# Moving and stationary tiles placed 192 bytes apart modulo 256 in an attention and two-layer expert kernel

## The chip, the cores and the metric

One NeuronCore of a Trainium2 chip runs the whole program. The metric is the device time of one execution in microseconds; the time before is 1484.91 us, the median of three runs (1484.45 to 1487.26).

## The reference

```python
# attention over keys and values averaged in groups of 8 (576 -> 72), for 8 batches and 8 heads of 64
scores = q @ mean8(k).T / 8;  attn = softmax(scores);  x = attn @ mean8(v)     # q, k, v: (8, 8, 576, 64)
x = x.transpose(0, 2, 1, 3).reshape(4608, 512)
# part one: three-way maximum, then a projection, d_ff = 768
h = maximum(maximum(x @ w1, x @ w2), x @ w3);  x = h @ w_out                    # 512 -> 768 -> 512
# part two: squared relu, d_ff = 2048
return ((relu(x @ w_in) ** 2) @ w_out)                                          # 512 -> 2048 -> 512
```

All inputs are float32; the weights arrive as 64-bit values that the kernel converts.

## The kernel before

Every large matrix product is made of three products of split values: an operand is cut into a high part (rounded to `float32r`) and the remainder, and high times high, high times low and low times high are summed in PSUM (`PARTS`). Each tile of activations or weights therefore has two halves, index 0 and 1. A matmul instruction names a stationary operand of 128 columns, which TensorE loads first (the profile's PEld rows), and a moving operand that is streamed past it (the PE rows). Every matmul has its own load.

Part one runs over 12 blocks of 384 tokens (`moe1`). A block does 18 products of 12 matmuls (L521: six chunks of the hidden layer times three weights; stationary `w1`, moving `x`, 384 columns) and 4 products of 18 matmuls (L540; stationary `wo1`, moving `h`). In a product the moving tile changes after every three matmuls. Attention for the next block (L361 to L421) and the preparation of part two's weights are woven between these steps by a table of due times.

Part two runs over 9 blocks of 512 tokens in a seven-product scheme on 2x2 blocks. `product` (L676) multiplies one of seven combinations of the activations, `y1` to `y7` (moving, 256 columns), with weights `wi2s` (stationary), 12 matmuls each. `moe2_out` (L806) has it the other way round: the split hidden values `g` are stationary and the output weights `wo2s`, fetched through a ring of five buffers, are the moving operand, 256 columns, again 12 matmuls with one `g` and one `wo2s`. Both lines have 3024 matmuls in all.

A scheduler sets the order of the instructions of every engine. Tiles are laid out by pools, one after the other along a partition of SBUF. What matters below is where a tile starts modulo 256 bytes; all slices of one tile that matmuls use start at the same place modulo 256, since the steps inside a tile are multiples of 512 bytes. Called *the difference* from here on: start of the moving operand minus start of the stationary operand, modulo 256. Before the change a helper, `shifted` (L90), allocates 16 floats more than a tile needs, so that neighbouring buffers of `x`, `h`, `y` and `wo2s` start 64 bytes apart modulo 256. Laid out by the pools, the starts modulo 256 are:

| operand | line | role | start before | difference before (matmuls) |
|---|---|---|---|---|
| `x` | L521 | moving | 160, 96, 32, 224 in turn | 0, 192, 128, 64 (648 each) |
| `w1`, `wo1` | L521, L540 | stationary | 160 | |
| `h` | L540 | moving | 160, 224, 96, 32 | 0 (300), 64 (276), 192 (156), 128 (132) |
| `y1` to `y7` | L676 | moving | 32, 32, 160, 96, 224, 96, 160 | 0 (864), 128 (864), 192 (810), 64 (486) |
| `wi2s` | L676 | stationary | 160, the first pair's half 32 | |
| `wo2s` | L806 | moving | 64, 64, 0, 192, 128 over the ring | 192 (1224), 0, 64, 128 (600 each) |
| `g` | L806 | stationary | 128 | |

So in L521 the difference changes after every three matmuls, and in part two it stays for stretches of 4 to 24 matmuls, since the scheduler weaves products in pieces of 4, 8 and 12.

Of the kernel before, what the change touches and what calls it, by code (L numbers as in the profile page):

```python
# [10 lines left out]
F32 = mybir.dt.float32  # L11
F32R = mybir.dt.float32r
# [8 lines left out]
P = 128  # L21
# [12 lines left out]
T1 = 384  # L34
# [29 lines left out]
AHEAD = 2  # L64
# [18 lines left out]
def as_f32(ap):  # L83
    return ap.bitcast(F32)


SHIFT = 16


def shifted(pool, shape, **names):  # L90

    n = 1
    for s in shape[1:]:
        n *= s
    t = pool.tile([P, n + SHIFT], F32R, **names)
    axes = " ".join(f"a{i}" for i in range(len(shape) - 1))
    return t[:, :n].rearrange(f"p ({axes}) -> p {axes}", **{f"a{i}": s for i, s in enumerate(shape[1:])})


@with_exitstack  # L100
def attention_moe_kernel(ctx: ExitStack, tc: tile.TileContext, q, k, v, vn, w1, w2, w3, wo1, wi2, wo2, out):
# [42 lines left out]
    def split(hl, src, engine=nc.vector):  # L144

        split_to(hl[:, 0], hl[:, 1], src, engine)
# [39 lines left out]

    w_p = s1.enter_context(tc.tile_pool(name="w_p", bufs=1))
    x_p = s1.enter_context(tc.tile_pool(name="x_p", bufs=2 * KD))
    h_p = s1.enter_context(tc.tile_pool(name="h_p", bufs=KF1))
    t_p = s1.enter_context(tc.tile_pool(name="t_p", bufs=2))  # L190

# [3 lines left out]
    sm_p = s_at.enter_context(tc.tile_pool(name="sm_p", bufs=4, side="right"))  # L195
    pt_p = s_at.enter_context(tc.tile_pool(name="pt_p", bufs=2, side="right"))
    xf_p = s_at.enter_context(tc.tile_pool(name="xf_p", bufs=1, side="right"))
    ah_p = s_at.enter_context(tc.tile_pool(name="ah_p", bufs=AHEAD, side="right"))
    sc_ps = s_at.enter_context(tc.tile_pool(name="sc_ps", bufs=2, space=PSUM))
    tr_ps = s_at.enter_context(tc.tile_pool(name="tr_ps", bufs=1, space=PSUM))  # L200
# [23 lines left out]
    unused = list(spare)  # L224
# [55 lines left out]
    x_t = {}  # L280
# [46 lines left out]
    def attend(j, b, s0, n, p, t):  # L327
# [23 lines left out]
        m = tiles[0][1]  # L351
# [46 lines left out]

        def values():
            if t == 0:  # L400
                x_t[j][p] = shifted(x_p, [P, 2, T1], tag="x", name="x")
            x = x_t[j][p][:, :, t : t + n]
            if whole:
                av = av_ps.tile([P, T1], F32, tag="av0", name="av0")[:, :n]
                for h in range(2):
                    nc.tensor.matmul(
                        av, lhsT=vst_f[p // 2][:, p % 2, h : h + 2].rearrange("p a d -> p (a d)"), rhs=pt[0][:, h, :n],
                        start=(h == 0), stop=(h == 1),
                    )
                split(x, av)  # L410
                return
            hi, lo = pt[0][:, 0, :, :n], pt[0][:, 1, :, :n]
            xf = xf_p.tile([P, T1], F32, tag="xf", name="xf")[:, :n]
            for h in range(2):
                av = av_ps.tile([P, T1], F32, tag=f"av{h}", name=f"av{h}")[:, :n]
                lhsT = vst[:, p, 2 * h : 2 * h + 2].rearrange("p a d -> p (a d)")
                nc.tensor.matmul(av, lhsT=lhsT, rhs=hi[:, h], start=True, stop=False)  # L417
                nc.tensor.matmul(av, lhsT=lhsT, rhs=lo[:, h], start=False, stop=True)  # L418
                r, o = slice(h * D, (h + 1) * D), slice((1 - h) * D, (2 - h) * D)
                nc.scalar.activation(xf[r], av[o], AF.Copy)  # L420
                nc.vector.tensor_tensor(out=xf[r], in0=av[r], in1=xf[r], op=ALU.add)  # L421
            split(x, xf)
# [86 lines left out]
    def moe1(j):  # L509

        x = x_t.pop(j)
        hs = []
        for f in range(KF1):
            hm = t_p.tile([P, T1], F32, tag="hm", name="hm")
            h = shifted(ah_p if j == 1 and f < AHEAD else h_p, [P, 2, T1], tag="h", name="h")
            for e in range(NE):
                ps = mm_ps.tile([P, T1], F32, tag="ps", name="ps")
                n = 0
                for kk in range(KD):
                    for a, c in PARTS:  # L520
                        nc.tensor.matmul(  # L521
                            ps, lhsT=w1_t[f, e][:, a, kk * P : (kk + 1) * P], rhs=x[kk][:, c],
                            start=(n == 0), stop=(n == 3 * KD - 1),
                        )
                        n += 1
                if e == 0:
                    nc.scalar.activation(hm, ps, AF.Copy)
                else:
                    nc.vector.tensor_tensor(out=hm, in0=ps, in1=hm, op=ALU.max)  # L529
                if e == NE - 1:  # L530
                    split(h, hm)
                yield
            hs.append(h)
            now[0] = hm
        for d in range(KD):
            ps = mm_ps.tile([P, T1], F32, tag="ps", name="ps")
            n = 0
            for kk in range(KF1):
                for a, c in PARTS:
                    nc.tensor.matmul(  # L540
                        ps, lhsT=wo1_t[kk][:, a, d * P : (d + 1) * P], rhs=hs[kk][:, c],
                        start=(n == 0), stop=(n == 3 * KF1 - 1),
                    )
                    n += 1
            ys = t_p.tile([P, T1], F32, tag="ys", name="ys")
            nc.scalar.activation(ys, ps, AF.Copy)
            nc.scalar.dma_start(out=y_dram[j][d], in_=ys)
            yield
# [6 lines left out]
    def add_moe1(j):  # L555
        steps = moe1(j)
        for i in range(STEPS):
            when = j * STEPS + i
            if j == 1 and i < NE * AHEAD:
                when = NE * KF1 + i * KD / (NE * AHEAD)  # L560
            todo.append((when, functools.partial(next, steps, None)))
# [31 lines left out]
    NG = NP2 // 2  # L593
    HT = T2 // 2
    y_p = ctx.enter_context(tc.tile_pool(name="y_p", bufs=1, side="right", reuse_waits="tile"))
    w2_p = ctx.enter_context(tc.tile_pool(name="w2_p", bufs=1, side="right", reuse_waits="tile"))
    wi2_t, wo2_t, yr_t, y_t = {}, {}, {}, {}

# [5 lines left out]
            wi2_t[p].append(w)  # L604

    def fetch_out(gr, m, h):
        w = shifted(wo_p, [P, 2, 2, 256], tag="wo2", name="wo2s")
        nc.sync.dma_start(out=as_f32(w), in_=wo2_dram[m, gr % 2, h])
        wo2_t.setdefault((gr, m, h), []).append(w)

# [30 lines left out]
    def split_y(j, m):  # L641
        src = y_t[j]
        if m == 4:
            src[4] = yr_t[j, 1, 0]
            nc.vector.tensor_tensor(out=src[4], in0=src[4], in1=as_f32(src["t6"]), op=ALU.subtract)
        if m == 6:
            src["t6"] = src[6]
        y = shifted(y_p, [P, 2, 2, HT], tag=f"y{m}", name=f"y{m}")
        split(y, src[m])
        src[m] = y  # L650

    ORDER = (1, 6, 7, 5, 2, 4, 3)
    early = [functools.partial(load_y, 0), functools.partial(mix_y, 0)]
    early.append(functools.partial(fetch_in, 0, w2_p))
    early += [functools.partial(split_y, 0, m) for m in ORDER]
    for i, f in enumerate(early):
        todo.append(((NB1 - 1) * STEPS + (i + 0.5) * (NE * KF1) / len(early), f))
# [4 lines left out]
    c_p = ctx.enter_context(tc.tile_pool(name="c_p", bufs=1, reuse_waits="tile"))  # L662
    w3_p = ctx.enter_context(tc.tile_pool(name="w3_p", bufs=1, reuse_waits="tile"))
    wo_p = ctx.enter_context(tc.tile_pool(name="wo_p", bufs=5, reuse_waits="tile"))
    for pool in (w3_p, wo_p):
        pool.tile([P, SHIFT // 2], F32, name="shift")
    acc_ps = ctx.enter_context(tc.tile_pool(name="acc_ps", bufs=1, space=PSUM, reuse_waits="tile"))

    def product(bank, j, gr, m, first=False):
# [145 lines left out]
    def fetch_group(gr):  # L815
        for m, h in OUT[gr >= NG // 2]:
            fetch_out(gr, m, h)
# [5 lines left out]
    for j in range(NB2):  # L823
        for gr in range(NG):
            more = j + 1 < NB2
            c = moe2_in(j, gr)

            ready = list(ORDER) if gr == NG - 1 and more else []
            for n, (m, h) in enumerate(OUT[gr >= NG // 2]):
                if n == 6 and ready:  # L830
                    mix_y(j + 1)
                if n >= 6:
                    for y in ready[2 * n - 12 : 2 * n - 10]:
                        split_y(j + 1, y)
                moe2_out(j, gr, m, h, c)
            if gr == NG - 2 and more:
                load_y(j + 1)
            nxt = j * NG + gr + 1
            if nxt < NB2 * NG:
                fetch_group(nxt % NG)  # L840
# [41 lines left out]
```

## Time and profile before

| | |
|---|---|
| median of three runs | 1484.91 us |
| the profiled execution | 1485.27 us |
| its span, first to last instruction | 1483.5 us |
| PE busy | 1452.1 us, 98% of the span |
| PEld, DVE, ACT, POOL busy | 96%, 66%, 52%, 12% |
| granted TensorE clock, mean over the span | 0.993 |
| part one, first matmul of L521 to last of L540 | 27.7 to 757.7 us |
| part two, L676 and L806 | 757.9 us to the end |

Matmuls overlap: the profile models the end of each, so a row's "mean ns of one" is longer than the step from one matmul's start to the next. The step is read from the timeline, as the distance of two rows' starts divided by the count.

### The profile page before, as it was taken

The page shows a single profiled execution, that of the slowest core. Times are in us where ns is not written, and L with a number is a line of the kernel's source. Part 1 is how long each engine was busy: PE and PEld are TensorE (multiplying, and loading weights), DVE is VectorE, ACT ScalarE, POOL GpSimd, SP SyncE. Part 2 cuts the span into 40 slices and gives each one's busy share as a digit, 9 for nine tenths or more (in the row PEclk, how much of TensorE's full clock was granted, in tenths as well). Part 3 has the DMA queues.
Part 4 walks back from the last instruction along what each step waited for, and adds up shares of the span by engine and source line. Part 5 has one row for each costly group of instructions (what it writes and reads, how often), then busy time and mean ns, then how long its engine had stood idle before and what let it go on. Part 6 is the DMA issues. An engine that isn't in the chain of part 4 may idle for free.

```text
span 1483.5 us, 27579 instructions
## 1 busy us (share of the span) xinstructions
PE 1452.1 (98%) x10410; PEld 1429.8 (96%) x10410; DVE 985.1 (66%) x1778; ACT 764.6 (52%) x1983; POOL 180.2 (12%) x228
## 2 busy tenths in 40 slices
PE   6889999999999999999999999999999999999998
PEld 4879999999999999999999999999999999999998
DVE  5896466675675756755426767676867767686765
ACT  7795365665666656654224544453635344454443
POOL 3441022312222212222000000000000000000000
PEclk9999999999999999999999999999999999999999
DMA  6643135533444433324369748475656666565746
GB/s 224 190 162 103 54 132 158 174 97 133 159 148 141 135 127 119 108 100 152 112 235 340 270 139 291 140 266 189 223 192 216 223 227 223 203 205 186 265 135 220
DMA packets 118307, 263.94 MB, mean 178 GB/s; under 512 B 12672, under 2 KB 62848, under 8 KB 118176
## 3 DMA queue, kind: packets, MB, share of 16 engines
q1 hardware_dynamic: 111264, 252.75, 50.4%
q10 hardware_dynamic: 6912, 9.44, 1.7%
q8 instruction: 82, 1.34, 0.4%
q14 instruction: 49, 0.40, 0.1%
HBM read 213.91 MB, written 48.23 MB: 177 GB/s over the span
## 4 chain that ended last, share of the span: by engine, by line
PE 90%; DMA 4%; ACT 3%; DVE 2%; issue 1%; POOL 0%; DVEq 0%; ACTq 0%; SPq 0%; POOLq 0%
PE ps L521 28%; PE ps L676 24%; PE ps L540 10%; PE accB L806 7%; PE accA L806 6%; PE accF L806 3%; PE accE L806 3%; PE accD L806 3%; PE sc L361 2%; DMA wo2s<-wo_dram 2%; PE tr L389 2%; ACT ss L366 1%; PE av L418 1%; DMA wraw<-in_w_dram 1%; PE av L417 1%
## 5 line engine op out<-in xcount | busy, mean ns | idle before, releaser
L521 PE MATMUL ps<-x,w 128*128 128x384 f32 x2592 | 496.1, 343 | 4.0 <-ACT w L141 1.3
L521 PEld LDWEIGHTS ps<-x,w 128*128 128x128 f32 x2592 | 451.9, 189 | 6.8 <-ACT w L141 3.0
L676 PE MATMUL ps<-y,wi2s 128*128 128x256 f32 x3024 | 378.8, 280 | 0.3
L676 PEld LDWEIGHTS ps<-y,wi2s 128*128 128x128 f32 x3024 | 365.6, 188 | 1.3 <-DVE a L686 0.6
L540 PE MATMUL ps<-h,wo 128*128 128x384 f32 x864 | 161.8, 339 | 0.2 <-ACT wo L141 0.2
L540 PEld LDWEIGHTS ps<-h,wo 128*128 128x128 f32 x864 | 149.6, 188 | 0.9 <-ACT wo L141 0.5
L686 DVE TENSOR_TENSOR c<-ps,c 128x512 f32<-128x512 f32 x144 | 98.4, 688 | 73.8 <-PE ps L676 72.5
L695 ACT ACTIVATE c<-c 128x512 f32<-128x512 f32 x90 | 55.7, 627 | 172.5 <-DVE c L686 170.3
L529 DVE TENSOR_TENSOR hm<-ps,hm 128x384 f32<-128x384 f32 x144 | 79.5, 552 | 69.4 <-PE ps L521 67.0
L141 ACT ACTIVATE g<-c 128x512 fp32r<-128x512 f32 x144 | 90.4, 627 | 59.2 <-DVE c L692 23.8
L806 PE MATMUL accB<-wo2s,g 128*128 128x256 f32 x864 | 115.5, 281 | 5.0 <-DMA wo2s<-wo_dram 3.5
L806 PE MATMUL accA<-wo2s,g 128*128 128x256 f32 x864 | 119.3, 280 | 0.0
L806 PEld LDWEIGHTS accB<-wo2s,g 128*128 128x128 f32 x864 | 107.3, 188 | 6.5 <-ACT g L141 3.2
L142 DVE TENSOR_TENSOR g<-c,g 128x512 fp32r<-128x512 f32 x144 | 98.6, 685 | 19.1 <-ACT g L141 19.1
L806 PEld LDWEIGHTS accA<-wo2s,g 128*128 128x128 f32 x864 | 109.6, 189 | 0.0
L366 ACT ACTIVATE ss<-sc,st 128x72 f32<-128x72 f32 (+1 forms) x320 | 97.9, 320 | 16.6 <-DVE st L363 14.1
L372 POOL TENSOR_TENSOR ss<-ss,st 128x432 f32<-128x432 f32 (+1 forms) x64 | 56.4, 881 | 261.7 <-DVE st L371 188.5
L421 DVE TENSOR_TENSOR xf<-av,xf 64x192 f32<-64x192 f32 (+1 forms) x112 | 50.7, 453 | 47.0 <-ACT xf L420 45.0
L393 DVE TENSOR_TENSOR pt<-tr,pt 72x192 fp32r<-72x192 f32 (+1 forms) x112 | 49.4, 450 | 41.2 <-ACT pt L392 39.4
L420 ACT ACTIVATE xf<-av 64x192 f32<-64x192 f32 (+1 forms) x112 | 45.4, 405 | 54.9 <-PE av L418 39.7
L141 ACT ACTIVATE h<-hm 128x384 fp32r<-128x384 f32 x72 | 37.6, 522 | 66.4 <-DVE hm L529 65.8
L141 ACT ACTIVATE g<-s 128x512 fp32r<-128x512 f32 x72 | 45.0, 630 | 45.4 <-DVE s L689 25.9
(105 smaller groups left out, 1980.8 us busy)
## 6 DMA issues: line engine op xcount, KB each, us to landing
wo2s<-wo_dram SPq DMA_DIRECT2D x252, 512.0 KB, 5.0
wi2s<-wi_dram SPq DMA_DIRECT2D x24, 512.0 KB, 9.0
wraw<-in_wo_dram SPq DMA_DIRECT2D x22, 512.0 KB, 4.3
wraw<-in_w_dram SPq DMA_DIRECT2D x18, 512.0 KB, 3.5
y_dram<-ys ACTq DMA_DIRECT2D x48, 192.0 KB, 2.0
wraw<-in_wi_dram SPq DMA_DIRECT2D x16, 512.0 KB, 3.8
wi_dram<-wraw SPq DMA_DIRECT2D x16, 512.0 KB, 3.6
wo_dram<-wraw SPq DMA_DIRECT2D x64, 128.0 KB, 2.0
```

The lines of the kernel that those rows point to most:

```text
L141: nc.scalar.activation(hi, src, AF.Copy)
L142: engine.tensor_tensor(out=lo, in0=src, in1=as_f32(hi), op=ALU.subtract)
L366: nc.scalar.activation(ss[:, i, h], src[:, i, h], AF.Exp, bias=st[:, 0, i, h : h + 1], accum_out=st[:, 1, i, h : h + 1],)
L372: nc.gpsimd.tensor_tensor(out=ss, in0=ss, in1=st[:, 2].rearrange("p g (h o) -> p g h o", o=1).to_broadcast([m, g, 2, SP]), op=ALU.mult,)
L421: nc.vector.tensor_tensor(out=xf[r], in0=av[r], in1=xf[r], op=ALU.add)
L521: nc.tensor.matmul(ps, lhsT=w1_t[f, e][:, a, kk * P : (kk + 1) * P], rhs=x[kk][:, c], start=(n == 0), stop=(n == 3 * KD - 1),)
L529: nc.vector.tensor_tensor(out=hm, in0=ps, in1=hm, op=ALU.max)
L540: nc.tensor.matmul(ps, lhsT=wo1_t[kk][:, a, d * P : (d + 1) * P], rhs=hs[kk][:, c], start=(n == 0), stop=(n == 3 * KF1 - 1),)
L676: nc.tensor.matmul(bank[:, u * HT : (u + 1) * HT], lhsT=wi2_t[2 * gr + u][i][:, a, o + kk * P : o + (kk + 1) * P], rhs=y_t[j][m][:, c, kk] ...
L686: nc.vector.tensor_tensor(out=out, in0=in0, in1=in1, op=ALU.add)
L695: nc.scalar.activation(c, c, AF.Relu)
L806: nc.tensor.matmul(bank[:, i * 256 : (i + 1) * 256], lhsT=g[:, a, u * HT + i * P : u * HT + (i + 1) * P], rhs=w[:, u, c], start=(n == 0 an ...
```

## The change

Instead of a longer tile, each pool gets one small tile that nothing uses (`leave`), which pushes what follows by 32 to 192 bytes. The tiles have their plain lengths again, all multiples of 512 bytes, so that all buffers of a pool start at the same place modulo 256. The starts become: `x` and `h` 96 against `w1` and `wo1` 160; `y1` to `y7` 224 against `wi2s` 32; `wo2s` 64 against `g` 128. Each of these differences is 192. The 32 small matmuls of L406 (first batch's attention values) go from a difference of 192 to 128.

The program keeps every instruction: on all five engines the same instructions with the same waits stand in the same order as before. Only addresses in SBUF differ.

```diff
--- before.py
+++ after.py
@@ -84,17 +84,9 @@
     return ap.bitcast(F32)
 
 
-SHIFT = 16
-
-
-def shifted(pool, shape, **names):
-
-    n = 1
-    for s in shape[1:]:
-        n *= s
-    t = pool.tile([P, n + SHIFT], F32R, **names)
-    axes = " ".join(f"a{i}" for i in range(len(shape) - 1))
-    return t[:, :n].rearrange(f"p ({axes}) -> p {axes}", **{f"a{i}": s for i, s in enumerate(shape[1:])})
+def leave(pool, size):
+
+    pool.tile([P, size // 4], F32, name="unused", bufs=1)
 
 
 @with_exitstack
@@ -186,6 +178,7 @@
 
     w_p = s1.enter_context(tc.tile_pool(name="w_p", bufs=1))
     x_p = s1.enter_context(tc.tile_pool(name="x_p", bufs=2 * KD))
+    leave(x_p, 192)
     h_p = s1.enter_context(tc.tile_pool(name="h_p", bufs=KF1))
     t_p = s1.enter_context(tc.tile_pool(name="t_p", bufs=2))
 
@@ -195,6 +188,7 @@
     sm_p = s_at.enter_context(tc.tile_pool(name="sm_p", bufs=4, side="right"))
     pt_p = s_at.enter_context(tc.tile_pool(name="pt_p", bufs=2, side="right"))
     xf_p = s_at.enter_context(tc.tile_pool(name="xf_p", bufs=1, side="right"))
+    leave(xf_p, 128)
     ah_p = s_at.enter_context(tc.tile_pool(name="ah_p", bufs=AHEAD, side="right"))
     sc_ps = s_at.enter_context(tc.tile_pool(name="sc_ps", bufs=2, space=PSUM))
     tr_ps = s_at.enter_context(tc.tile_pool(name="tr_ps", bufs=1, space=PSUM))
@@ -398,7 +392,7 @@
 
         def values():
             if t == 0:
-                x_t[j][p] = shifted(x_p, [P, 2, T1], tag="x", name="x")
+                x_t[j][p] = x_p.tile([P, 2, T1], F32R, tag="x", name="x")
             x = x_t[j][p][:, :, t : t + n]
             if whole:
                 av = av_ps.tile([P, T1], F32, tag="av0", name="av0")[:, :n]
@@ -512,7 +506,7 @@
         hs = []
         for f in range(KF1):
             hm = t_p.tile([P, T1], F32, tag="hm", name="hm")
-            h = shifted(ah_p if j == 1 and f < AHEAD else h_p, [P, 2, T1], tag="h", name="h")
+            h = (ah_p if j == 1 and f < AHEAD else h_p).tile([P, 2, T1], F32R, tag="h", name="h")
             for e in range(NE):
                 ps = mm_ps.tile([P, T1], F32, tag="ps", name="ps")
                 n = 0
@@ -593,6 +587,7 @@
     NG = NP2 // 2
     HT = T2 // 2
     y_p = ctx.enter_context(tc.tile_pool(name="y_p", bufs=1, side="right", reuse_waits="tile"))
+    leave(y_p, 192)
     w2_p = ctx.enter_context(tc.tile_pool(name="w2_p", bufs=1, side="right", reuse_waits="tile"))
     wi2_t, wo2_t, yr_t, y_t = {}, {}, {}, {}
 
@@ -604,7 +599,7 @@
             wi2_t[p].append(w)
 
     def fetch_out(gr, m, h):
-        w = shifted(wo_p, [P, 2, 2, 256], tag="wo2", name="wo2s")
+        w = wo_p.tile([P, 2, 2, 256], F32R, tag="wo2", name="wo2s")
         nc.sync.dma_start(out=as_f32(w), in_=wo2_dram[m, gr % 2, h])
         wo2_t.setdefault((gr, m, h), []).append(w)
 
@@ -645,7 +640,7 @@
             nc.vector.tensor_tensor(out=src[4], in0=src[4], in1=as_f32(src["t6"]), op=ALU.subtract)
         if m == 6:
             src["t6"] = src[6]
-        y = shifted(y_p, [P, 2, 2, HT], tag=f"y{m}", name=f"y{m}")
+        y = y_p.tile([P, 2, 2, HT], F32R, tag=f"y{m}", name=f"y{m}")
         split(y, src[m])
         src[m] = y
 
@@ -662,8 +657,8 @@
     c_p = ctx.enter_context(tc.tile_pool(name="c_p", bufs=1, reuse_waits="tile"))
     w3_p = ctx.enter_context(tc.tile_pool(name="w3_p", bufs=1, reuse_waits="tile"))
     wo_p = ctx.enter_context(tc.tile_pool(name="wo_p", bufs=5, reuse_waits="tile"))
-    for pool in (w3_p, wo_p):
-        pool.tile([P, SHIFT // 2], F32, name="shift")
+    leave(w3_p, 160)
+    leave(wo_p, 32)
     acc_ps = ctx.enter_context(tc.tile_pool(name="acc_ps", bufs=1, space=PSUM, reuse_waits="tile"))
 
     def product(bank, j, gr, m, first=False):
```

## Rows read from the trace of the kernel before

**Rows 1.** The page: busy time by engine; the chain that ended last, by engine.

```profile
PE 1452.1 (98%) x10410; PEld 1429.8 (96%) x10410; DVE 985.1 (66%) x1778; ACT 764.6 (52%) x1983; POOL 180.2 (12%) x228
...
PE 90%; DMA 4%; ACT 3%; DVE 2%; issue 1%; POOL 0%; DVEq 0%; ACTq 0%; SPq 0%; POOLq 0%
```

**Rows 2.** Busy time by stretch, all engines, with granted clock and DMA share.

```profile
core 0: us, PE busy (x) PEld busy (x) DVE busy (x) ACT busy (x) POOL busy (x), PEclk, DMA share, GB/s
400.00:600.00 200.00, 200.00 (x1224) 198.41 (x1224) 127.28 (x275) 120.69 (x402) 46.15 (x65) 1.00 0.43 140
900.00:1100.00 200.00, 199.82 (x1698) 199.47 (x1697) 146.91 (x233) 92.01 (x160) 0.00 (x0) 1.00 0.63 218
```

**Rows 3.** Groups of matmuls by line, whole span: xcount | busy us, mean ns | idle us.

```profile
L521 PE MATMUL ps<-x,w 128*128 128x384 f32 x2592 | 496.1, 343 | 4.0 <-ACT w L141 1.3 <-DVE hm L529 1.0 <-ACT hm L527 0.8
L676 PE MATMUL ps<-y,wi2s 128*128 128x256 f32 x3024 | 378.8, 280 | 0.3
L540 PE MATMUL ps<-h,wo 128*128 128x384 f32 x864 | 161.8, 339 | 0.2 <-ACT wo L141 0.2
L806 PE MATMUL accA<-wo2s,g 128*128 128x256 f32 x864 | 119.3, 280 | 0.0
L806 PE MATMUL accB<-wo2s,g 128*128 128x256 f32 x864 | 115.5, 281 | 5.0 <-DMA wo2s<-wo_dram 3.5 <-ACT qB L769 0.7 <-ACT g L141 0.6
```

**Rows 4.** Same view, L676 from 782.30, 783.08, 818.42, 820.07 us: differences 192, 0, 64, 128.

```profile
L676 PE MATMUL ps<-y,wi2s 128*128 128x256 f32 x7 | 1.0, 276 | 0.0
...
L676 PE MATMUL ps<-y,wi2s 128*128 128x256 f32 x12 | 1.6, 281 | 0.0
...
L676 PE MATMUL ps<-y,wi2s 128*128 128x256 f32 x12 | 1.6, 279 | 0.0
...
L676 PE MATMUL ps<-y,wi2s 128*128 128x256 f32 x10 | 1.3, 281 | 0.0
```

**Rows 5.** Same view, L806 from 799.17 and 776.41 us: differences 0, 64.

```profile
L806 PE MATMUL accA<-wo2s,g 128*128 128x256 f32 x12 | 1.6, 283 | 0.0
...
L806 PE MATMUL accB<-wo2s,g 128*128 128x256 f32 x12 | 1.6, 279 | 0.0
```

**Rows 6.** Same view, L806 from 801.00 and 857.87 us: difference 192 both times.

```profile
L806 PE MATMUL accB<-wo2s,g 128*128 128x256 f32 x12 | 1.5, 276 | 0.0
...
L806 PE MATMUL accB<-wo2s,g 128*128 128x256 f32 x24 | 3.0, 281 | 0.0
```

**Rows 7.** Timeline of PE, L806 at difference 192, each time with the next row.

```profile
start us, us, engine line op out<-in xcount [idle before <-releaser]
973.70 1.53 PE L806 MATMUL accF<-wo2s,g 128*128 128x256 f32 x12
975.06 0.52 PE L676 MATMUL ps<-y,wi2s 128*128 128x256 f32 x3
...
857.62 2.99 PE L806 MATMUL accB<-wo2s,g 128*128 128x256 f32 x24
860.46 0.40 PE L676 MATMUL ps<-y,wi2s 128*128 128x256 f32 x2
```

**Rows 8.** Groups by line, 1346.5 to 1348.1 us: L676, then L806, both at 192.

```profile
L676 PE MATMUL ps<-y,wi2s 128*128 128x256 f32 x8 | 1.1, 276 | 0.0
...
L806 PE MATMUL accA<-wo2s,g 128*128 128x256 f32 x8 | 1.1, 281 | 0.0
```

**Rows 9.** Groups, 384 columns, from 306.70, 171.50, 163.10 us: mixed, 192, 0.

```profile
L521 PE MATMUL ps<-x,w 128*128 128x384 f32 x12 | 2.3, 336 | 0.0
...
L540 PE MATMUL ps<-h,wo 128*128 128x384 f32 x6 | 1.2, 334 | 0.0
...
L540 PE MATMUL ps<-h,wo 128*128 128x384 f32 x6 | 1.2, 341 | 0.0
```

**Rows 10.** Longest waits of PE, 755 to 1483: us, times, longest; landing of wo2s.

```profile
PE accB L806 <- DMA wo2s<-wo_dram: 3.5, 3, 1.6
...
DMA to landing us min/median/max: 3.2/5.0/8.0
```

## The prediction

> **What bounds the kernel now.** I read the page's busy time first, then the busy time by stretch, then the groups of matmuls. PE is busy 98% of the span and makes up 90% of the chain that ended last; DMA has 4% of it [rows 1]. In the middle of part one, 400 to 600 us, PE is busy for all of 200 us, in part two for 199.82 of 200, at a granted clock of 1.00, which is the 2.4 GHz level; DVE, the next engine, has 146.91 of 200 [rows 2]. So the time is the number of matmuls times the step from one to the next, and nothing else is near to being late.
>
> Four lines carry it: L521 (2592 matmuls) and L540 (864) with 384 columns, L676 (3024) and L806 (3024) with 256 [rows 3]. The change touches no instruction, only where operands start, so the question is whether a matmul's step depends on the difference of its two operands' starts. The trace before can answer that, since it holds all four differences side by side, for the same shapes on the same lines.
>
> It does depend. A row's mean is longer than the step by a constant: at 276 ns the step is (975.06 - 973.70) / 12 = 113.3 ns, at 281 ns (860.46 - 857.62) / 24 = 118.3 ns, both times 163 ns less [rows 6, 7]. A nanosecond less in the mean is a nanosecond less in the step. On L676 stretches at difference 192, 0, 64 and 128 have means of 276, 281, 279 and 281 [rows 4]; on L806 differences 0 and 64 have 283 and 279 [rows 5]. Only 192 reaches 276.
>
> But 192 does not always reach it. The stretch of L806 from 857.87 us is at 192 as well, 24 matmuls long, and stays at 281 to its end; the one from 801.00 is at 276 [rows 6]. So there are two rhythms at 192, a settled one (step 113.3) and an unsettled one (118.3), and a stretch keeps the one it has fallen into. The change of line is where it falls: at 1347.24 us, with 192 on both sides, L676 leaves at 276 and L806 goes on at 281 [rows 8]. This is the last of nine such crossings out of twelve that ended in the slow rhythm. Stretches at 192 that follow another difference settle more often than not, and take some five matmuls for it.
>
> **The change part by part.** It removes no instruction, adds none, and no engine's order or wait moves. What it does is to make every difference on the four lines 192.
>
> *Part two.* The means are 280 on L676 and 280 to 281 on L806 [rows 3], say 280.2. Were every matmul at 276, the gain would be 4.2 ns x 6048 = 25.4 us. Were every one in the slow rhythm at 281, it would be a loss of 0.8 x 6048 = 4.8 us (the means are rounded, so 0 to 5). Which of the two it is hangs on what a crossing from L676 to L806 and back does, for after the change these are the only breaks left. Before, three of twelve crossings with 192 on both sides settled; entered from other differences, most stretches did. The pair of starts that meets at a crossing is a new one (224 against 128 and 64 against 32; before 96 against 128 and 64 against 160), so the trace has no like case. I take a half: mean 278.5, a gain of 1.7 x 6048 = 10.3 us.
>
> *Part one.* Here the difference changes after every three matmuls, so there are no long stretches. A whole product of L521, three matmuls at each of the four differences, has a mean of 336; six matmuls of L540 at 192 have 334, and six at 0, just behind attention's matmuls, 341 [rows 9]. (The means of the whole lines, 343 and 339 [rows 3], hold those that follow a stall or another line; these stay.) From 336 the bounds are 2 ns x 3456 = 6.9 us of gain and 5 x 3456 = 17.3 us of loss. I take 1 ns, 3.5 us: 334 is one calm stretch, and the other breaks, attention's matmuls between the products, stay as they are.
>
> *L406.* 32 small matmuls go from 192 to 128; at the 5 ns between the rhythms this is 0.2 us at most, so nothing.
>
> *The fetches.* `wo2s` comes through a ring of five, and a fetch is issued when the matmuls that read the buffer are done. While L806 runs alone, four other products cover it: 4 x 12 x 117.3 ns = 5.6 us now, 5.5 us at the step I expect, 5.4 us if all settles, against a landing of 5.0 us in the median and 8.0 at most; PE waits 3.5 us for it on one bank today [rows 10]. Some of the gain comes back as wait: I take 0.5 us. DVE and ACT have room [rows 1, 2].
>
> *Sum.* 10.3 + 3.5 - 0.5 = 13.3 us. The profiled execution took 1485.27 us, 0.36 over the median of the three runs: 1485.27 - 13.3 = 1472.0, and 1471.6 on the median's scale.
>
> *A rule against the change.* The trace shows means from 276 to 283 for one shape at one clock [rows 4, 5]. The Trainium skill, "TensorE: Matmul & The Clock Gate", section "Step-by-step: what each phase is for", says that TensorE has two independent read ports, one for the streamed operand and one for the weights, and that loading the next weights does not take read bandwidth from the running matmul. By that the starts of the two should not matter to each other, and the time would be that of before; the rows speak against it, though what in the engine makes the difference no row shows.
>
> **The rivals.**
>
> *Everything settles.* Part two runs at 276 throughout: 25.4 us, with 3.5 of part one 28.9. The first matmuls behind each crossing will still be slow, so some 2 us less: 1458. For it: stretches that follow another difference mostly settle, as that of L806 from 801.00 does behind one at 0 [rows 5, 6]. Against it: nine of twelve crossings [rows 8].
>
> *Nothing settles.* With 192 everywhere, each crossing throws the next stretch into the slow rhythm, and no other difference comes along to shake it out; the slow rhythm lasted 24 matmuls without breaking [rows 6]. Part two then gains nothing and may lose up to 4.8 us, part one gives 3.5: 1481 to 1486, in the middle 1483.
>
> *The starts don't matter.* What looks like the difference is the place in the schedule (a product's neighbours, its bank), and moves with it: 1484.9. Against it: the same levels on two lines whose operands have opposite roles [rows 4 to 6].
>
> *Part one falls into a slow rhythm.* The 341 of six matmuls at difference 0 [rows 9] shows that 384 columns have one too. Today the difference changes every three matmuls, which breaks it up; with one difference it could last for a whole block. At 341 it costs 17.3 us, against the 10.3 - 0.5 of part two: 1485 + 17.3 - 9.8 = 1492. It decides for slower from a mean of about 339 on, where 3456 matmuls at 3 ns lose what part two gains. Against it: at 192 the stretch that I can read is at 334.
>
> **How the numbers follow.** The mixed case (half settled) has 0.50, everything settles 0.20, nothing settles 0.14, no dependence 0.07, the slow part one 0.09. A measurement of this kernel can tell about 0.2%, or 3 us, from no change. The mixed case and everything settled are faster; of "nothing settles" 0.06 is faster and 0.08 within 3 us, where the case of no dependence lies as well: faster 0.76, same 0.15, slower 0.09. The likeliest case alone goes from 1464 to 1479 (a quarter to three quarters settled in part two: 2.7 to 17.8 us there instead of 10.3). The range takes in everything settled and nothing settled, 1457 to 1486; outside remain most of the slow case and a part one that gains 6.9 beside a settled part two.
>
> **What will show it.** In the profile after, the means of L676 and of L806's banks should stand near 278 to 279: 276 to 277 is the first rival, 280 to 281 the second or third. In the timeline of part two, stretches of L676 and L806 should have steps of either 113.3 or 118 and hardly the 120 of today's difference 0. A product of L521 should have 335; 339 and over is the slow case. PE's wait for `wo2s` should be 4 to 6 us. The forecast is wrong if part two's means do not move, if the gain comes from part one, or if a wait for DMA grows by more than 2 us.

## The result, and the profile after

The changed kernel takes 1468.95 us (median of four runs, 1466.55 to 1474.21); the kernel before, beside it, 1486.09 us (four runs). The ratio is 0.9886, 95% interval 0.9848 to 0.9923. Two executions among the runs below, one of 2876 us and one of 3625 us, are left out of the ratios. The profiled execution took 1471.22 us with a span of 1469.4 us, 14.1 less than before. Lines have moved by five to six: L521 is now L515, L540 is L534, L676 is L671, L806 is L801.

The page first: busy time by engine, and the shares of the chain that ended last.

```profile
PE 1432.7 (98%) x10410; PEld 1408.8 (96%) x10410; DVE 985.2 (67%) x1778; ACT 764.8 (52%) x1983; POOL 183.0 (12%) x228
...
PE 87%; DMA 6%; ACT 3%; DVE 3%; issue 1%; POOL 0%; SPq 0%; DVEq 0%; ACTq 0%; POOLq 0%
```

Against [rows 1] PE has lost 19.4 us of busy time with the same number of instructions, and DMA's share of the chain has gone from 4% to 6%. The stretches by engine:

```profile
core 0: us, PE busy (x) PEld busy (x) DVE busy (x) ACT busy (x) POOL busy (x), PEclk, DMA share, GB/s
400.00:600.00 200.00, 200.00 (x1223) 198.42 (x1222) 127.21 (x270) 120.92 (x403) 47.27 (x65) 1.00 0.43 141
900.00:1100.00 200.00, 198.62 (x1734) 197.96 (x1733) 148.79 (x236) 93.57 (x162) 0.00 (x0) 1.00 0.64 221
```

In part one PE does as many matmuls in 200 us as before (1223 against 1224), in part two 1734 against 1698, at the same granted clock [rows 2]. So the gain is part two's. The groups of matmuls (count, busy, mean ns of one, idle before them):

```profile
L515 PE MATMUL ps<-x,w 128*128 128x384 f32 x2592 | 494.1, 342 | 4.9 <-ACT w L133 2.2 <-DVE hm L523 1.1 <-POOL w L134 0.8
L671 PE MATMUL ps<-y,wi2s 128*128 128x256 f32 x3024 | 368.5, 277 | 0.4 <-DVE a L681 0.2
L534 PE MATMUL ps<-h,wo 128*128 128x384 f32 x864 | 163.9, 342 | 2.3 <-POOL wo L134 1.8 <-ACT wo L133 0.5
L801 PE MATMUL accA<-wo2s,g 128*128 128x256 f32 x864 | 116.3, 277 | 0.1
L801 PE MATMUL accB<-wo2s,g 128*128 128x256 f32 x864 | 112.6, 278 | 5.4 <-DMA wo2s<-wo_dram 3.9 <-ACT g L133 0.8 <-ACT qB L764 0.7
```

Part two's means went from 280 to 277 on L671 and from 280 and 281 to 277 and 278 on L801; part one's did not fall (342 and 342, before 343 and 339) [rows 3]. The view of a line's instructions gives the shortest, median and longest, and the starts of the first and the last; here L521 and L676 of before, and the same lines of after.

```profile
L521 PE MATMUL ps<-x,w x2592: 331/337/1095, 27.7 to 745.2; 128*128 128x384 f32 x200
...
L676 PE MATMUL ps<-y,wi2s x3024: 274/280/390, 757.9 to 1463.3; 128*128 128x256 f32 x189
```

```profile
L515 PE MATMUL ps<-x,w x2592: 331/336/994, 27.7 to 747.3; 128*128 128x384 f32 x200
...
L671 PE MATMUL ps<-y,wi2s x3024: 275/276/394, 759.9 to 1449.9; 128*128 128x256 f32 x189
```

Part two starts at 759.9 us where it started at 757.9, so part one has become 2 us longer and part two, to the end of the span, 16 us shorter. More than half of all matmuls of L671 are now at 276 or less. The timeline of PE at the beginning of part two shows stretches that are settled, and stay so over the crossings from line to line:

```profile
start us, us, engine line op out<-in xcount [idle before <-releaser]
773.04 1.53 PE L801 MATMUL accA<-wo2s,g 128*128 128x256 f32 x12
774.40 0.86 PE L671 MATMUL ps<-y,wi2s 128*128 128x256 f32 x6
775.11 1.52 PE L801 MATMUL accA<-wo2s,g 128*128 128x256 f32 x12
776.47 2.89 PE L801 MATMUL accB<-wo2s,g 128*128 128x256 f32 x24
779.19 0.52 PE L671 MATMUL ps<-y,wi2s 128*128 128x256 f32 x3
```

The 12 matmuls of L801 from 773.04 take 1.36 us to the next row, 113.3 ns a step, those from 776.47 2.72 us for 24, the same; six of L671 between them take 0.71 us (118) and do not throw the next stretch off. That is the settled step of [rows 7]. Counted from the starts, 182 stretches of at least eight matmuls follow a crossing of lines in part two; 166 of them hold no wait (no step over 150 ns), and 165 of these run at 113.3 from their sixth matmul on. What is left of the second half of [rows 6] comes behind waits, as here, where PE waited 0.69 us in the middle of a long stretch of L801:

```profile
806.56 1.68 PE L801 MATMUL accB<-wo2s,g 128*128 128x256 f32 x12 [0.69 <-ACT qB L764]
808.08 1.58 PE L801 MATMUL accA<-wo2s,g 128*128 128x256 f32 x12
809.49 1.58 PE L801 MATMUL accE<-wo2s,g 128*128 128x256 f32 x12
```

From 808.08 to 809.49 us the step is 117.5 ns, at the same difference of 192. Of the 27 waits with at least seven matmuls of the same line behind them, 11 leave the line at some 118 ns and 16 at 113.3; the 11 have 265 matmuls behind them, some 1.2 us in all at 4.5 ns each. Taken from all starts (each to the next start of the same line, those over 150 ns left out as stalls), the step went from 117.6 to 113.9 ns on L671 and from 117.4 to 114.0 on L801.

Part one has two sorts of products now. One stretch of L515 in the middle, and one from the last block, which has no attention woven in:

```profile
L515 PE MATMUL ps<-x,w 128*128 128x384 f32 x13 | 2.5, 338 | 0.0
...
L515 PE MATMUL ps<-x,w 128*128 128x384 f32 x89 | 15.6, 335 | 0.0
```

At 335 the step is 173.3 ns, at 338 it is 176.7; over the part the steps are 175.2 (L515) and 175.6 (L534), before 175.1 and 174.6. The waits of PE for a fetch have grown (total us, times, longest), with hardly a change in the landing:

```profile
PE accB L801 <- DMA wo2s<-wo_dram: 3.9, 6, 1.3
PE accF L801 <- DMA wo2s<-wo_dram: 1.9, 2, 1.2
PE accE L801 <- DMA wo2s<-wo_dram: 0.5, 1, 0.5
```

```profile
DMA to landing us min/median/max: 3.2/5.1/8.2
```

On the bank that had 3.5 us in three waits [rows 10] it is 3.9 in six, on two others 2.4 us, where the kernel before has 0.8 on one:

```profile
PE accF L806 <- DMA wo2s<-wo_dram: 0.8, 2, 0.4
```

In all it is 6.3 us where it was 4.3.

### The profile page after: what moved, and what is told of

It reads as the page before. It is cut to its first block, busy times and chain, and to the rows that moved or that the text cites. A ratio compares the mean times of both kernels' runs of the same rounds, so it can differ in the third digit from the quotient of the medians.

```text
span 1469.4 us, 27579 instructions
## 1 busy us (share of the span) xinstructions
PE 1432.7 (98%) x10410; PEld 1408.8 (96%) x10410; DVE 985.2 (67%) x1778; ACT 764.8 (52%) x1983; POOL 183.0 (12%) x228
## 4 chain that ended last, share of the span: by engine, by line
PE 87%; DMA 6%; ACT 3%; DVE 3%; issue 1%; POOL 0%; SPq 0%; DVEq 0%; ACTq 0%; POOLq 0%
PE ps L515 28%; PE ps L671 22%; PE ps L534 10%; PE accB L801 6%; PE accA L801 6%; DMA wo2s<-wo_dram 4%; PE accF L801 3%; PE accE L801 3%; PE sc L355 2%; PE tr L383 2%; PE accD L801 2%; PE av L412 1%; PE av L411 1%; DMA vr<-in_v_dram 1%; ACT ss L360 1%
## 5 line engine op out<-in xcount | busy, mean ns | idle before, releaser
L515 PE MATMUL ps<-x,w 128*128 128x384 f32 x2592 | 494.1, 342 | 4.9 <-ACT w L133 2.2
L515 PEld LDWEIGHTS ps<-x,w 128*128 128x128 f32 x2592 | 450.1, 189 | 7.8 <-ACT w L133 4.3
L671 PE MATMUL ps<-y,wi2s 128*128 128x256 f32 x3024 | 368.5, 277 | 0.4 <-DVE a L681 0.2
L671 PEld LDWEIGHTS ps<-y,wi2s 128*128 128x128 f32 x3024 | 355.2, 188 | 1.4 <-DVE a L681 0.7
L534 PE MATMUL ps<-h,wo 128*128 128x384 f32 x864 | 163.9, 342 | 2.3 <-POOL wo L134 1.8
L534 PEld LDWEIGHTS ps<-h,wo 128*128 128x128 f32 x864 | 151.2, 189 | 3.0 <-POOL wo L134 2.2
L801 PE MATMUL accB<-wo2s,g 128*128 128x256 f32 x864 | 112.6, 278 | 5.4 <-DMA wo2s<-wo_dram 3.9
L801 PE MATMUL accA<-wo2s,g 128*128 128x256 f32 x864 | 116.3, 277 | 0.1
L801 PEld LDWEIGHTS accB<-wo2s,g 128*128 128x128 f32 x864 | 104.5, 188 | 7.2 <-ACT g L133 4.0
L801 PEld LDWEIGHTS accA<-wo2s,g 128*128 128x128 f32 x864 | 107.2, 188 | 0.3 <-ACT g L133 0.3
L134 DVE TENSOR_TENSOR h<-hm,h 128x384 fp32r<-128x384 f32 x72 | 48.9, 679 | 26.1 <-ACT h L133 25.6
```

The lines of the kernel that those rows point to most:

```text
L134: engine.tensor_tensor(out=lo, in0=src, in1=as_f32(hi), op=ALU.subtract)
L515: nc.tensor.matmul(ps, lhsT=w1_t[f, e][:, a, kk * P : (kk + 1) * P], rhs=x[kk][:, c], start=(n == 0), stop=(n == 3 * KD - 1),)
L534: nc.tensor.matmul(ps, lhsT=wo1_t[kk][:, a, d * P : (d + 1) * P], rhs=hs[kk][:, c], start=(n == 0), stop=(n == 3 * KF1 - 1),)
L671: nc.tensor.matmul(bank[:, u * HT : (u + 1) * HT], lhsT=wi2_t[2 * gr + u][i][:, a, o + kk * P : o + (kk + 1) * P], rhs=y_t[j][m][:, c, kk] ...
L801: nc.tensor.matmul(bank[:, i * 256 : (i + 1) * 256], lhsT=g[:, a, u * HT + i * P : u * HT + (i + 1) * P], rhs=w[:, u, c], start=(n == 0 an ...
```

## The experiments

Two theories stand against each other. The first: a matmul's step depends on the difference of the two operands' starts, line by line. The second: what counts is that the difference no longer changes from stretch to stretch, whatever it is. A third question is what became of part one. In all kernels but the one with six buffers the engines' instructions are those of the changed kernel, in the same order; only the sizes of unused tiles differ, or, in the first two, which tiles come from `shifted`. The kernel before took 1490 to 1492 us on the chips of these runs, so ratios are compared, not times.

**Part two alone** (`part_two_only`): x and h come from `shifted` again.

```diff
-                x_t[j][p] = x_p.tile([P, 2, T1], F32R, tag="x", name="x")
+                x_t[j][p] = shifted(x_p, [P, 2, T1], tag="x", name="x")
-            h = (ah_p if j == 1 and f < AHEAD else h_p).tile([P, 2, T1], F32R, tag="h", name="h")
+            h = shifted(ah_p if j == 1 and f < AHEAD else h_p, [P, 2, T1], tag="h", name="h")
-    leave(x_p, 192)
-    leave(xf_p, 128)
```

> Part one is laid out as before (x and h 64 bytes apart from buffer to buffer), part two as after (difference 192 on both lines). If the gain is part two's alone, this kernel takes what the changed kernel takes, 1467 to 1470 us, with means of 277 on part two's two lines and 336 to 337 in part one's calm products. If part one's new layout gives its forecast 3.5 us, this one is 3 to 4 us slower than the changed kernel, about 1472.

Measured: 1476.88 us, ratio 0.9903 (0.9874 to 0.9931). That is the changed kernel's gain within the intervals; a second measurement of the changed kernel (below) has 0.9895. A difference of some 4 us could not be told from these times.

**Part one alone** (`part_one_only`): `y` and `wo2s` come from `shifted` again, x and h are as after.

```diff
-    leave(y_p, 192)
...
-        w = wo_p.tile([P, 2, 2, 256], F32R, tag="wo2", name="wo2s")
+        w = shifted(wo_p, [P, 2, 2, 256], tag="wo2", name="wo2s")
...
-        y = y_p.tile([P, 2, 2, HT], F32R, tag=f"y{m}", name=f"y{m}")
+        y = shifted(y_p, [P, 2, 2, HT], tag=f"y{m}", name=f"y{m}")
...
-    leave(w3_p, 160)
-    leave(wo_p, 32)
+    for pool in (w3_p, wo_p):
+        pool.tile([P, SHIFT // 2], F32, name="shift")
```

> Part one is laid out as after (difference 192 for x and h), part two as before. If part one gains nothing, the time is that of before within 3 us (1484 to 1488), with means of 280 in part two. If part one gains its forecast 3.5 us, 1481 to 1482. If a slow rhythm costs part one something, 1488 or more.

Measured: 1491.67 us, ratio 1.0001 (0.9986 to 1.0016). Nothing gained. The lines' views (shortest, median, longest; first and last start) of the projection line of part one and of part two's first line, first in this kernel, then in the one with part two alone:

```profile
L547 PE MATMUL ps<-h,wo x864: 331/338/669, 101.6 to 760.9; 128*128 128x384 f32 x173
...
L683 PE MATMUL ps<-y,wi2s x3024: 274/280/390, 761.0 to 1469.5; 128*128 128x256 f32 x189
```

```profile
L545 PE MATMUL ps<-h,wo x864: 331/336/442, 100.3 to 757.2; 128*128 128x384 f32 x173
...
L682 PE MATMUL ps<-y,wi2s x3024: 276/276/394, 757.4 to 1452.6; 128*128 128x256 f32 x189
```

With part one at 192 its projections have a median of 338 instead of 336, and part two begins at 761.0 instead of 757.4 us. Part two has 280 with its old layout and 276 with the new one. So the whole gain is part two's, and part one's new layout costs some 2 to 3.6 us in the profile, too little for the timings to tell.

**One difference everywhere, but another** (`zero`, `sixtyfour`, `two24`, `one60`, and `others`, with 32 on L672 and L535 and 96 on L516 and L802): the sizes of the unused tiles alone, for difference 0 for instance

```diff
-    leave(x_p, 192)
-    leave(xf_p, 128)
+    leave(xf_p, 64)
-    leave(y_p, 192)
+    leave(y_p, 256)
-    leave(w3_p, 160)
-    leave(wo_p, 32)
+    leave(w3_p, 352)
+    leave(wo_p, 160)
```

> All four lines at one difference again, but at 0 instead of 192. If the step hangs on the difference, part two's lines have means of 281 to 283 (steps of 118 to 120), and the time is 5 to 6 ns x 6048 = 30 to 37 us over the changed kernel: 1499 to 1506. If it is the sameness that counts (no change of difference from stretch to stretch), whatever the difference, the means are 277 and the time 1469. For part one both leave 173 to 177 ns a step.

> All four lines at difference 64. If the step hangs on the difference, part two's lines have a mean of 279 to 280 (step 117.5), 3.5 ns x 6048 = 21 us over the changed kernel: about 1490. If sameness counts alone, 277 and 1469.

> All four lines at difference 224. If only the residue in steps of 64 counts (which quarter of 256 bytes), 224 behaves as 192: means of 277 in part two. If the step follows the difference more finely, its means lie between those at 192 (277) and at 0 (283), about 280, and the time near that of before.

> All four lines at difference 160. By quarters of 256 bytes it behaves as 128: means of 281 in part two, time about that of before. If the best place is a broad one around 192, 160 has 277 to 279 and a time near the changed kernel's.

> The differences not yet seen: L671 and the projection line of part one at 32, L801 and the first line of part one at 96. If 192 is the one good place for 256 columns, both lines of part two have means of 279 to 283. If there are others, one of them is at 277.

Measured: difference 0 takes 1499.26 us, 1.0071 times before (1.005 to 1.0091); 64 takes 1482.51, 224 takes 1490.94, 160 takes 1489.34 and the mixed pair 1495.35 us in single runs beside 1490.41, 1492.08, 1492.08 and 1490.68 of before. The lines of part two (shortest, median, longest) at 0, at 64, at 224 and at 160:

```profile
L670 PE MATMUL ps<-y,wi2s x3024: 277/283/387, 755.6 to 1475.6; 128*128 128x256 f32 x189
...
L800 PE MATMUL accA<-wo2s,g x864: 277/283/331, 769.1 to 1482.3; 128*128 128x256 f32 x173
```

```profile
L671 PE MATMUL ps<-y,wi2s x3024: 276/279/388, 755.1 to 1460.5; 128*128 128x256 f32 x189
...
L801 PE MATMUL accA<-wo2s,g x864: 275/279/392, 768.4 to 1466.8; 128*128 128x256 f32 x173
L801 PE MATMUL accB<-wo2s,g x864: 276/276/383, 771.9 to 1472.2; 128*128 128x256 f32 x173
```

```profile
L671 PE MATMUL ps<-y,wi2s x3024: 274/280/388, 756.8 to 1466.7; 128*128 128x256 f32 x189
```

```profile
L671 PE MATMUL ps<-y,wi2s x3024: 276/281/388, 755.5 to 1467.5; 128*128 128x256 f32 x189
```

and at 32 (L672) and 96 (L802):

```profile
L672 PE MATMUL ps<-y,wi2s x3024: 275/280/390, 761.5 to 1471.3; 128*128 128x256 f32 x189
...
L802 PE MATMUL accA<-wo2s,g x864: 276/281/329, 774.8 to 1478.0; 128*128 128x256 f32 x173
```

The median is 283 at 0, where sameness alone asks for 276: the second theory falls. 160 behaves as a quarter of 256 bytes would have it (281, as 128 before), but 224, only 32 bytes from 192, has 280, so quarters don't decide either. L801 at 64 has banks at 276 and banks at 279: two rhythms again. The mean steps, taken as above from all starts (stalls over 150 ns, with 384 columns over 230 ns, left out), with the kernel that gave them:

| difference | L671, 256 columns | L801, 256 columns | L515, 384 columns | L534, 384 columns | kernel |
|---|---|---|---|---|---|
| 0 | 119.8 | 119.5 | 174.6 | 174.0 | `zero` |
| 32 | 116.7 | | | 174.7 | `others` |
| 64 | 117.7 | 115.7 | 173.6 | 173.6 | `sixtyfour` |
| 96 | | 119.8 | 176.9 | | `others` |
| 128 | | | 176.2 | 176.3 | `moved` |
| 160 | 118.3 | 118.1 | 174.0 | 173.9 | `one60` |
| 192 | 113.9 | 114.0 | 175.2 | 175.6 | changed kernel |
| 224 | 118.3 | 118.2 | 174.3 | 174.1 | `two24` |
| mixed | 117.6 | 117.4 | 175.1 | 174.6 | before |

Where the table is empty, nothing was measured. The columns are headed by the changed kernel's lines; in the kernels `zero`, `others` and before the same lines have other numbers. For 256 columns 192 is the best of the places tried, by 1.7 to 6 ns; for 384 columns it is worse than 0, 64, 160 and 224, and 64 is the best.

The time at 0 rose less than was expected (30 to 37 us over the changed kernel): by the ratios it is 26 to 28 us. On L670 and L800 the steps are 5.9 and 5.5 ns longer, 34 us; but part two begins at 755.6 us where it begins at 759.9 in the changed kernel, and PE stalls less for the fetches: 12.6 us of part two are stalls, 14.4 in the changed kernel's profile. The two profiles' spans differ by 26.5 us; they are of different chips, and the kernel before differs by some 4 us between these.

**Other places, the same difference** (`moved`): `wo2s` and `g` both start 64 bytes further on. Part one goes to difference 128 in the same kernel, for the table.

```diff
-    leave(x_p, 192)
+    leave(x_p, 128)
...
-    leave(xf_p, 128)
+    leave(xf_p, 192)
...
-    g_p = ctx.enter_context(tc.tile_pool(name="g_p", bufs=4, reuse_waits="tile"))
+    g_p = ctx.enter_context(tc.tile_pool(name="g_p", bufs=4, reuse_waits="tile")); leave(g_p, 64)
...
-    leave(w3_p, 160)
-    leave(wo_p, 32)
+    leave(w3_p, 96)
+    leave(wo_p, 96)
```

> The changed kernel with both operands of L801 moved by 64 bytes (wo2s starts at 128, g at 192; the difference stays 192), and part one at difference 128. If the difference decides, L801 keeps its mean of 277 and its step of 114; if the places themselves do, it changes, to 279 or more. Part one at 128 fills in its table: the stretches of three before stood at 176, the others so far went from 173.6 (64) to 175.3 (192).

Measured: 1477.6 us in one run beside 1490.68 of before. L801's line:

```profile
L801 PE MATMUL accA<-wo2s,g x864: 276/276/384, 775.9 to 1462.3; 128*128 128x256 f32 x173
```

The median is still 276, the step 114.3. So it is the difference that counts, not where the two lie; shown by a move for L801 alone. L671, with its operands at other places again (224 and 32), has the same step at 192. This kernel also changes the pair of starts that meets at a crossing in part two, with both lines still at 192: 162 of its 167 stretches of at least eight matmuls without a wait settle.

That the place counts modulo 256 bytes, and not 512, can be read for L806 from the trace before. The two buffers of `wo2s` whose difference was 192 lie 65 times 256 bytes apart, and both have products that end at the settled step: 17 of 23 and 13 of 22 of those that could be read, against 2 of 63 on the other three buffers (products given to buffers in the program's order).

**Part one at 64, part two at 192** (`one_at_64`), first by itself, then beside the changed kernel on one chip:

```diff
-    leave(x_p, 192)
+    leave(x_p, 64)
-    leave(xf_p, 128)
+    leave(xf_p, 256)
```

> The changed kernel with x and h at difference 64 instead of 192; part two stays at 192. With all four lines at 64, part one's stream stepped at 173.6 ns against 175.2 to 175.6 at 192. If the step hangs on the difference line by line, this kernel has part two's means at 277 and part one's calm products at 335 to 336, and is 1.6 to 2 ns x 3456 = 5.5 to 7 us faster than the changed kernel; against before some 1.3 to 1.4% faster. If part one is bound by attention's chain and not by its matmuls, the gain turns into waits and the time is the changed kernel's.

> The changed kernel itself, timed beside the next one on the same chip. About 0.987 of before by what has been measured so far.

> Part one at difference 64, part two at 192. In the profile of its first run part one took 727.6 us against 732.2 for the changed kernel; if that holds, the ratio to before is 0.003 to 0.004 lower than that of the changed kernel beside it. If the two are equal, the 4.6 us were the two chips' difference or came back as wait.

Measured: 1469.10 us, ratio 0.9847 (0.9824 to 0.9870). In the second job 1470.84 us, 0.9862 (0.9841 to 0.9882), beside 1474.62 us, 0.9895 (0.9873 to 0.9916) for the changed kernel. The lines that begin and end part one in the two profiles of that job:

```profile
L515 PE MATMUL ps<-x,w x2592: 331/336/1095, 27.8 to 746.3; 128*128 128x384 f32 x200
...
L671 PE MATMUL ps<-y,wi2s x3024: 275/276/394, 759.0 to 1449.4; 128*128 128x256 f32 x189
```

```profile
L515 PE MATMUL ps<-x,w x2592: 331/336/1095, 27.7 to 742.2; 128*128 128x384 f32 x200
...
L671 PE MATMUL ps<-y,wi2s x3024: 275/276/388, 754.9 to 1446.7; 128*128 128x256 f32 x189
```

L671 begins at 754.9 instead of 759.0 us, 4.1 earlier (755.4 in the first job's profile); the steps are 173.6 on both lines of part one, at 114 part two is unchanged. By the steps 1.6 x 2592 + 1.9 x 864 = 5.8 us were to be had. The medians of the second job differ by 3.8 us, as this asks for, but the two intervals overlap: that the version is faster than the changed kernel is seen in the profiles, and only likely by the times. By its ratio it is the fastest of all that ran.

**A sixth buffer for `wo2s`** (`one_at_64_ring6`), on top of that:

```diff
-    g_p = ctx.enter_context(tc.tile_pool(name="g_p", bufs=4, reuse_waits="tile"))
+    g_p = ctx.enter_context(tc.tile_pool(name="g_p", bufs=3, reuse_waits="tile"))
-    wo_p = ctx.enter_context(tc.tile_pool(name="wo_p", bufs=5, reuse_waits="tile"))
+    wo_p = ctx.enter_context(tc.tile_pool(name="wo_p", bufs=6, reuse_waits="tile"))
```

> The same, with six buffers in the wo2s ring and three instead of four for g (the space of a partition is used up). If the added waits for wo2s come from the ring's depth, PE's wait for wo2s falls from 4 to 9 us to under 2 and the time by 3 to 6 us. If they come from late transfers as such, or if three g tiles now make PE wait for the split on ACT, nothing is gained, or the time grows by a few us.

Measured: 1474.05 us, ratio 0.9871 (0.9838 to 0.9904): no gain over the version with five. The longest waits of PE, in `one_at_64` and with the sixth buffer:

```profile
PE accB L801 <- DMA wo2s<-wo_dram: 8.0, 7, 2.4
```

```profile
PE accA L801 <- ACT g L133: 6.2, 7, 0.9
PE ps L671 <- DVE c L681: 4.9, 8, 1.6
PE accF L801 <- DMA wo2s<-wo_dram: 2.4, 3, 0.9
```

The wait for `wo2s` fell from 8.0 us on one bank to 2.4 on another, which points to the ring's depth. It is not shown alone, since this kernel's instructions also stand in another order (the scheduler saw other pools). With three tiles for `g` PE waits 6.2 us for the split on ACT and 4.9 us for DVE. Both at once do not fit into the partition, and a deeper ring beside four `g` was not tried.

## Why the prediction was right, and where it was not

The time lies 2.7 us below the forecast of 1471.6 us, and the way was the forecast's; against the kernel before beside it the gain is 17.1 us where 13.3 were forecast. But that the sum came so near is luck: two terms that were sized wrong nearly cancel. By the profiles part two became 16.1 us shorter where 10.3 - 0.5 = 9.8 were forecast, and part one 2.0 us longer where 3.5 us shorter was.

*Part two, "I take a half".* The mechanism was right: the step depends on the difference, and at 192 there is a settled rhythm. The size failed: nearly everything settled, which had been the first rival. The count of crossings that spoke against it does not come out of the trace. From the starts of all matmuls, 18 stretches of at least eight of L806 follow L676 with 192 on both sides; nine stay slow, as the prediction has it, but nine settle by their sixth matmul, not three. The six that come from a settled stretch of twelve of L676, as in [rows 8], all stay slow; after the change 165 of 166 settle. The pair of starts that meets at a crossing is another one, as the forecast said. That this is what helps is likely, since a third pair (`moved`) settles in 162 of 167 cases as well, but it is not shown: no kernel had 192 throughout part two with the old pair.

The gain adds up so. The 2880 steps inside L671 give 3.7 ns each, 10.7 us, and some 2850 inside L801 3.4 ns, 9.7 us, 20.4 in all. The step across a crossing from L671 to L801 became longer, 121.3 instead of 117.9 ns without the waits, 134 times: 0.5 us back. The waits take another 3.8, which leaves the 16.1 us. Also "only 192 reaches 276" was a reading of short stretches: at 64, L801 has banks at 276 too.

*The fetches, "I take 0.5 us".* Too small. Stalls in part two (what steps over 150 ns have beyond 116) went from 10.6 to 14.4 us, 3.8 more. Among the forecast's own signs of being wrong was a wait for DMA that grows by more than 2 us. Here it grew by 2.0, from 4.3 to 6.3 us, and in the other five profiles with part two at 192 and five buffers it is 7.1 to 10.5 us; in the profiles whose steps in part two are on the average no shorter than before it is 4.3 to 6.1 us. The margin of some 0.2 us that the faster step takes off the ring's cover was rightly worked out; that it would be missed this often was not. The kernel with six buffers points to the ring, with the limits named there.

*Part one, "I take 1 ns, 3.5 us".* This step failed. The calm stretch at 334 in [rows 9] was taken for what 192 does; the trace after has products at 335 and products at 338, and on the average it is no better than before. The rival of a slow rhythm in part one named the right thing at far too high a price: not 341 for a whole block, but 338 in a part of the products. Beside it PE waits more at the beginning, 2.3 us for the first projections' weights where it was 0.2 ([rows 3] and the groups after); why, no run shows.

*The rule against the change.* The Trainium skill, "TensorE: Matmul & The Clock Gate", section "Step-by-step: what each phase is for", says that loading the next weights takes no SBUF read bandwidth from the running matmul. Here the step of one and the same program goes from 113.9 to 119.8 ns with the difference of the two starts alone. Measurement decides: where the operands lie does matter. What inside the engine or the memory does it, these runs don't show.

*What the prediction lacked.* It had the steps of single stretches at all four differences, and read 192 as best for both shapes. For 384 columns the stretch at 192 that it read had six matmuls [rows 9], and so short a one said nothing about what the line settles into.

## What to carry to other kernels

Where matmuls with their own weight loads follow each other without a gap, as in this kernel, the place of the moving operand against the stationary one, modulo 256 bytes, was worth 5% of the step with 256 columns (113.9 to 119.8 ns) and 2% with 384 (173.6 to 176.9), and one unused tile in a pool sets it. The best place was not the same for the two widths: take one measurement for each line and width, with the difference held for the whole line, since short stretches show transitions and not the rhythm that it settles into. And when a bound engine gets faster by a few per cent, look at the rings that were just deep enough for it.

## What the runs showed of the hardware that was not expected

- A line at a fixed difference can have more than one steady rhythm. At 192 with 256 columns 113.3 and 118 ns both held to the end of stretches of 24 matmuls in the trace before; at 192 with 384 columns 173.3 and 176.7 stand beside each other in one run; at 64 L801 has banks at a median of 276 and of 279. A wait can move a line from one to the other: in the changed kernel L801 runs at 113.3 ns up to a wait at 805.6 us and at 117.8 behind it.
- The best difference is not the same with 256 and 384 columns: 192 gives the shortest step of those tried at 256 columns (113.9 ns) and one of the longer at 384 (175.2 to 175.6), where 64 has 173.6. The two lines of each width agree; the two parts differ in more than the width, so that it is the width is not shown.
- 32 bytes decide: 160 and 224 have 118.3 ns on L671, 192 between them 113.9.
